# A second MoE computed in two phases over all tokens, both by seven block products

## The chip, the cores and the metric

One core of one Trainium2 chip. The metric is the time of the device in microseconds, as the median of several executions. TensorE (PE) multiplies, with a stationary operand of at most 128 x 128 and a moving operand of at most 512 columns; VectorE (DVE) and ScalarE (ACT) work element by element; SyncE (SP) issues every transfer here, on one queue.

## The reference

Inputs are x (8 batches, 8 heads, 512 tokens, 64 features), 32 states per batch and head, and weights.

```
attention: xread = softmax(x state^T / 8) state      512 rows per batch and head
           sread = softmax(state x^T / 8) x           32 rows per batch and head
tokens  = both by batch: 8 x (512 + 32) = 4352 rows of 512 features
first MoE:  h = relu(tokens @ w_in)  (512 x 2048);   y = (h * h) @ w_out
second MoE: xn = y / sqrt(mean(y*y) + 1e-6) * rms_g
            g = xn @ w_gate;  v = xn @ w_val          (512 x 1536 each)
            out = (g * sigmoid(g) * v) @ w_out2       (1536 x 512)
```

The weights arrive as float64 and are turned into float32 on the chip. A float32 product runs as three float32r passes: each operand is split into hi and lo = value - hi, and hi*hi + hi*lo + lo*hi are accumulated in PSUM.

## The kernel before

Tokens are features by tokens on chip: 128 features on the partitions, tokens in the columns. There are nine blocks: the 512 tokens of each batch, and the 256 states of all batches together (the state block, `SB`). A chunk is 128 hidden features.

**Order.** Every step is put at a position with `put(pos, fn, ...)`, and all steps are issued sorted by position. The unit is one chunk of an MoE loop. Positions that are not fixed by the loops come from the table `T`. Each engine works through its instructions in this order, and waits inside a step hold up what stands behind it on that engine. SP's transfers are one queue in the same order.

**Buffers.** On-chip buffers are 54 slots of 4 KB per partition (`u(...)`, one [128, 2, 512] float32 each); a slot is used again when the last reader of its old tile is done. PSUM has eight banks, four under the tag "mm" and four under "acc"; each holds 512 float32 per partition.

**First MoE** (L441 to L532). `moe1_in` makes h of a chunk, ScalarE applies Relu and Square, and the result is split: hi by a VectorE copy at L467, lo by a subtraction at L468. `moe1_out` adds the chunk to four "acc" banks, 2.5 positions after the chunk's place. At the end of a block `moe1_fin0` copies the banks out, two on ScalarE (L494) and two on VectorE (L495); `moe1_sq`, `moe1_rms`, `moe1_rinv` and `moe1_norm` make the normalized tokens, which are stored to DRAM (`xn_dr`). During a batch the attention of the next one is computed in steps in between. The weights of the second MoE are loaded and turned into float32 words during batches 1 to 7, and stored to DRAM as these.

**Second MoE** (L552 to L704). Gate and value of a chunk are one product of 2 x 2 blocks: rows of gate and value, halves of the 512 features, halves of the block's 512 tokens. Seven block products (Winograd's form of Strassen's algorithm) replace eight. Each is two 128-row blocks by three passes, with 256 tokens moving: 42 matmuls of 256 columns a chunk (`moe2_in`). ScalarE copies the first product, VectorE adds the others from PSUM (L646), then SiLU (L660), gate times value (L663) and the split of the result. `moe2_out` multiplies by w_out2 without block products: 4 token groups x 3 passes, 12 matmuls of 512 columns, one chunk later. The state block uses 24 matmuls of 256 columns and 6 of 512.

Weights for six of the twelve chunks are on chip at a time, so all blocks are gone through twice: `order` lists (half, block), the first half leaves partial sums in DRAM (`part_dr`), the second adds to them and stores the output (`moe2_fin`, L696).

```
    order = [(0, blk) for blk in (0, 1, 2, 3, SB, 4, 5, 6, 7)]
    order += [(1, blk) for blk in (7, 0, 1, 2, SB, 3, 4, 5, 6)]
```

Of the kernel before, what the change touches and what calls it, by code (L numbers as in the profile page):

```python
# [55 lines left out]
def attention_moe_kernel(  # L56
# [30 lines left out]
    NFH = NF2 // 2  # L87
# [9 lines left out]
    serial = [0]  # L97

# [59 lines left out]
    # A pair is two [128, 512] blocks of a weight; words holds it as float32 bits.  # L158
# [16 lines left out]
    def conv_a(key, j):  # L175
        if (key, j) not in raws:
            return
        t = raws[key, j]
        nc.scalar.activation(f(words[key][:, j, :]), f(t[:, :, 1]), AF.Abs, scale=2.0**-80)  # L179
        nc.scalar.activation(t[:, :, 0], t[:, :, 0], AF.Copy, bias=LOW_BIAS, scale=LOW_SCALE)  # L180

    def conv_b(key, j):
        if (key, j) not in raws:
            return
        t = raws.pop((key, j))
        w = words[key][:, j, :]
# [11 lines left out]
    def load_words(key):  # L198
        words[key] = u([P, 2, 512], U32, "wd")
        nc.sync.dma_start(f(words[key]), dram_words(key))  # L200

    his = {}

    def hi_words(key):
        his[key] = u([P, 2, 512], F32R, "wh")
        nc.scalar.copy(his[key], f(words[key]))
# [41 lines left out]
    def p_store(fq, bp, g):  # L248
        t = pst.pop((fq, bp, g))
# [7 lines left out]
    def load_p(b, fq):  # L257
        t = u([P, 2, 512], F32, "praw")
# [17 lines left out]
    def attn_steps(b):  # L276
# [38 lines left out]
        def s_pd(fq, g):  # L315
            """One batch's product with w_in by groups of heads, kept on chip."""
# [13 lines left out]
        def s_ex(g):  # L330
            t = st[g]
# [29 lines left out]
        def s_tokb(g):  # L361
            t = tk[g]
# [16 lines left out]
        def s_e2t(hc):  # L379
            ps = bank("mm", "e2p")  # L380
# [11 lines left out]
        def s_at(g):  # L392
            t = tk.pop(g)
# [5 lines left out]
        def s_sr(g):  # L399
            ps = bank("mm", "srp")  # L400
# [17 lines left out]
        def s_srt():  # L418
            ps = bank("mm", "srt")
# [21 lines left out]
    def moe1_in(blk, fc):  # L441
# [25 lines left out]
        nc.vector.tensor_copy(t[:, 0, :n], rg[:, 1, :n])  # L467
# [21 lines left out]
    def moe1_fin0(blk):  # L489
        n = ntok[blk]  # L490
# [8 lines left out]
    def moe1_sq(blk):  # L499
        n = ntok[blk]  # L500
# [10 lines left out]
    def moe1_rms(blk):  # L511
        n = ntok[blk]
# [6 lines left out]
    def moe1_rinv(blk, h):  # L519
        n = ntok[blk] // 2  # L520
# [3 lines left out]
    def moe1_norm(blk, j):  # L524
        n = ntok[blk]
# [12 lines left out]
    wsp = {}  # L538
    wtmp = {}
    w2 = {}  # L540
    xload = {}
    xtmp = {}
    xsp = {}
    part = {}
    part_dr = [
        dram.tile([P, ntok[k] // P, DM], F32, tag=f"part{k}", name=f"part_dr{k}")
        for k in range(NB)
    ]
    W_NAMES = ("a11", "a12", "a22", "s1", "s2", "s3", "s4")
    X_NAMES = ("b11", "b21", "b22", "t1", "t2", "t3", "t4")  # L550
# [4 lines left out]
    def load_w(c2):  # L555
        load_words(("wg", c2))
        load_words(("wv", c2))

    def sums_w(c2):
        g = f(words.pop(("wg", c2)))  # L560
        v = f(words.pop(("wv", c2)))
        t = [u([P, 2, 512], F32, "ws") for _ in range(2)]
        s1, s2, s3, s4 = t[0][:, 0, :], t[0][:, 1, :], t[1][:, 0, :], t[1][:, 1, :]
        a11, a12, a21, a22 = g[:, 0, :], g[:, 1, :], v[:, 0, :], v[:, 1, :]
        nc.vector.tensor_tensor(s1, a21, a22, op=ALU.add)
        nc.vector.tensor_tensor(s3, a11, a21, op=ALU.subtract)
        nc.vector.tensor_tensor(s2, s1, a11, op=ALU.subtract)
        nc.vector.tensor_tensor(s4, a12, s2, op=ALU.subtract)
        wtmp[c2] = dict(a11=a11, a12=a12, a22=a22, s1=s1, s2=s2, s3=s3, s4=s4)

    def split_w(c2, name):
        src = wtmp[c2].pop(name)
        t = u([P, 2, 512], F32R, "wq")
        split(src, t[:, 0, :], t[:, 1, :])
        wsp[c2, name] = quads(t)

    def load_xn(blk, j):
        t = u([P, 2, 512], F32, "xld")
        nc.sync.dma_start(t[:, :, : ntok[blk]], xn_dr[blk][:, 2 * j : 2 * j + 2, :])
        xload[blk, j] = t  # L580

    def sums_x(blk):
        x1, x2 = xload.pop((blk, 0)), xload.pop((blk, 1))
        b11, b21 = x1[:, :, :256], x2[:, :, :256]
        if blk == SB:
            t = u([P, 2, 256], F32, "xt4")
            nc.vector.tensor_tensor(t, b21, b11, op=ALU.subtract)
            xtmp[blk] = dict(b11=b11, b21=b21, t4=t)
            return
# [374 lines left out]
```

## Time and profile before

| | |
|---|---|
| time, median of 3 runs | 1525.35 us (1524.79 to 1525.41) |
| span of the profiled execution (its own time between first and last instruction) | 1524.0 us |
| TensorE busy | 1492.9 us, 98% |
| TensorE weight loads busy | 1327.7 us, 87% |
| VectorE busy | 1162.4 us, 76% |
| ScalarE busy | 734.6 us, 48% |
| transfers | 165 MB, mean 108 GB/s |
| granted TensorE clock, mean | 0.991 of full |

A busy share is the part of the span in which at least one instruction of the engine ran. Matmuls overlap, so the duration of one is longer than the distance from one to the next. In a list of groups the columns are: line, engine, operation, tiles written and read, shape and count, then busy time, mean of one in ns, and the idle time of the engine before them with what ended it. The first MoE runs to about 713 us, the second from there to the end; the first 60 us hold the first loads and conversions.

### The profile page before, as it was taken

What the parts mean: (1) busy time and instruction counts of PE and PEld (TensorE: products, weight loads), DVE (VectorE), ACT (ScalarE), POOL (GpSimd) and SP (SyncE); (2) the same over time, 40 slices, a digit from 0 to 9 for tenths busy, and PEclk for the clock granted to TensorE, in tenths of its full rate; (3) what the DMA queues carried; (4) which work ended last, traced back from release to release, by engine and by line L of the source; (5) the groups of instructions that cost most, each with busy time, mean ns of one, the idle gap of its engine ahead of it and who ended that gap; (6) DMA issues with size and microseconds to landing.
All of it is one profiled execution on the core that took longest, in us unless ns stands there. A gap on an engine that the chain in (4) does not pass through costs nothing.

```text
span 1524.0 us, 22599 instructions
## 1 busy us (share of the span) xinstructions
PE 1492.9 (98%) x8858; PEld 1327.7 (87%) x8858; DVE 1162.4 (76%) x2186; ACT 734.6 (48%) x1263; POOL 0.7 (0%) x6
## 2 busy tenths in 40 slices
PE   4999999999999999999999999999999999999998
PEld 2788888888888888889899999999999999999998
DVE  7997788888888989678886655778677776576674
ACT  5998666667666667654532323334332332232231
POOL 0000000000000000000000000000000000000000
PEclk6999999999999999999999999999999999999999
DMA  8976251515251534313021102012312022212100
GB/s 316 366 229 216 95 201 70 214 57 212 84 206 64 215 108 180 139 42 112 14 70 56 42 30 83 31 53 75 121 55 83 15 84 70 83 48 78 56 28 29
DMA packets 54971, 165.04 MB, mean 108 GB/s; under 512 B 6224, under 2 KB 7760, under 8 KB 54864
## 3 DMA queue, kind: packets, MB, share of 16 engines
q1 hardware_dynamic: 54864, 163.60, 30.7%
q8 instruction: 69, 1.13, 0.3%
q14 instruction: 38, 0.31, 0.1%
HBM read 109.58 MB, written 54.00 MB: 107 GB/s over the span
## 4 chain that ended last, share of the span: by engine, by line
PE 93%; ACT 3%; DVE 3%; issue 0%; DMA 0%; ACTq 0%; DVEq 0%
PE o L118 14%; PE o L119 14%; PE o L120 14%; PE x L120 10%; PE x L119 10%; PE x L118 10%; PE h L119 4%; PE h L118 4%; PE h L120 4%; ACT pst L246 1%; PE pps L118 1%; PE pps L120 1%; PE pps L119 1%; ACT wd L179 1%; ACT raw L180 1%; PE srp L120 1%
## 5 line engine op out<-in xcount | busy, mean ns | idle before, releaser
L118 PE MATMUL x<-xs,wq 128*128 128x256 f32 x1344 | 380.0, 283 | 0.5 <-ACT sq L517 0.4
L120 PE MATMUL x<-xs,wq 128*128 128x256 f32 x1344 | 380.3, 283 | 0.0
L119 PE MATMUL x<-xs,wq 128*128 128x256 f32 x1344 | 380.3, 283 | 0.0
L118 PEld LDWEIGHTS x<-xs,wq 128*128 128x128 f32 x1344 | 257.6, 192 | 4.5 <-ACT sq L517 0.6
L119 PEld LDWEIGHTS x<-xs,wq 128*128 128x128 f32 x1344 | 257.6, 192 | 3.6
L120 PEld LDWEIGHTS x<-xs,wq 128*128 128x128 f32 x1344 | 257.6, 192 | 0.0
L118 PE MATMUL o<-hl,wh 128*128 128x512 f32 (+1 forms) x576 | 217.7, 378 | 0.0
L119 PE MATMUL o<-hl,wh 128*128 128x512 f32 (+1 forms) x576 | 217.4, 377 | 0.0
L120 PE MATMUL o<-hl,wl 128*128 128x512 f32 (+1 forms) x576 | 217.4, 377 | 0.0
L660 ACT ACTIVATE rg<-rg 128x512 f32<-128x512 f32 x96 | 60.7, 632 | 319.6 <-DVE rg L646 319.6
L646 DVE TENSOR_TENSOR q<-q,x 128x256 f32<-128x256 f32 x288 | 112.3, 417 | 92.5 <-ACT q L649 58.3
L646 DVE TENSOR_TENSOR rg<-q,x 128x256 f32<-128x256 f32 x384 | 147.0, 417 | 25.8 <-PE x L120 25.3
L118 PE MATMUL o<-wh,hl 128*128 128x512 f32 x408 | 160.2, 393 | 1.0 <-ACT x L494 1.0
L119 PE MATMUL o<-wl,hl 128*128 128x512 f32 x408 | 160.0, 392 | 0.0
L120 PE MATMUL o<-wh,hl 128*128 128x512 f32 x408 | 158.7, 389 | 0.0
L115 DVE TENSOR_TENSOR hl<-rg,hl 128x512 fp32r<-128x512 f32 (+1 forms) x108 | 71.6, 663 | 71.6 <-ACT hl L114 71.6
L120 PEld LDWEIGHTS o<-hl,wl 128*128 128x128 f32 x576 | 108.4, 188 | 20.1
L118 PEld LDWEIGHTS o<-hl,wh 128*128 128x128 f32 x576 | 108.4, 188 | 19.8
L119 PEld LDWEIGHTS o<-hl,wh 128*128 128x128 f32 x576 | 108.4, 188 | 19.6
L464 ACT ACTIVATE rg<-h 128x512 f32<-128x512 f32 (+1 forms) x144 | 82.2, 571 | 83.1 <-PE h L120 82.9
L114 ACT CAST hl<-rg 128x512 fp32r<-128x512 f32 (+1 forms) x108 | 64.4, 597 | 91.1 <-DVE rg L663 72.8
L118 PE MATMUL h<-at,ph 128*128 128x512 f32 x256 | 101.5, 397 | 2.7 <-ACT pst L246 2.7
(154 smaller groups left out, 2592.1 us busy)
## 6 DMA issues: line engine op xcount, KB each, us to landing
raw<-in_moe_w_out_dram SPq DMA_DIRECT2D x30, 512.0 KB, 8.9
xld<-xn_dr SPq DMA_DIRECT2D x30, 512.0 KB, 5.7
p_dr<-pst SPq DMA_DIRECT2D x56, 256.0 KB, 4.6
praw<-p_dr SPq DMA_DIRECT2D x28, 512.0 KB, 4.2
xr<-in_x_t_dram SPq DMA_DIRECT2D x16, 512.0 KB, 6.0
raw<-in_moe_w_in_dram SPq DMA_DIRECT2D x16, 512.0 KB, 9.6
x<-in_x_n_dram SPq DMA_DIRECT2D x16, 512.0 KB, 8.4
xn_dr<-x SPq DMA_DIRECT2D x16, 512.0 KB, 3.3
```

The costliest lines, as they stand in the source:

```text
L114: nc.scalar.copy(hi, src)
L115: nc.vector.tensor_tensor(lo, src, f(hi), op=ALU.subtract)
L118: nc.tensor.matmul(ps, lh, rh, start=start, stop=False)
L119: nc.tensor.matmul(ps, lh, rl, start=False, stop=False)
L120: nc.tensor.matmul(ps, ll, rh, start=False, stop=stop)
L179: nc.scalar.activation(f(words[key][:, j, :]), f(t[:, :, 1]), AF.Abs, scale=2.0**-80)
L180: nc.scalar.activation(t[:, :, 0], t[:, :, 0], AF.Copy, bias=LOW_BIAS, scale=LOW_SCALE)
L246: nc.scalar.copy(pst[fq, bp, g][:, q, :], ps)
L464: nc.scalar.activation(rg[:, 0, :n], ps[:, :n], AF.Relu)
L646: add = lambda o, a, ps: nc.vector.tensor_tensor(o, a, ps, op=ALU.add)
L660: nc.scalar.activation(rg[:, 0, :], rg[:, 0, :], AF.Silu)
```

## The change

Gate and value are now computed for all tokens first (phase one), and the output product for all tokens after that (phase two).

- Phase one goes over pairs of batches `s`: the token halves of the 2 x 2 product are two batches of 512 tokens, so that each product has 512 moving columns. A pair of column blocks (`c2`, 256 gate and value columns) is loaded, summed and split, from DRAM: 7 tiles of 512 KB, for each pair of batches again. The state block follows each chunk of the last pair.
- Results of two chunks are summed for the left side of the output product (`h_sums`) and stored in DRAM as seven blocks (`h_store`).
- Phase two does the output product by seven block products too: blocks of two chunks by two halves of the 512 output features, for the tokens of two batches. It needs seven PSUM banks, accumulated over six pairs of chunks. The split w_out2 stays on chip (24 tiles).
- Sums and splits of all three weights are made during the first MoE (`wq_sums`, `wq_split`, `w2_sums`, `w2_split`) and stored in DRAM ready to use.
- In the first MoE the hi copy at L467 goes to ScalarE for all blocks but the first, the output products of batches 1 to 7 are issued one chunk later, and the last output products of the state block are drawn closer together.
- `after(step, *needs)` asserts while the program is written that a step stands behind those it needs, norm and its reciprocals among them; it issues nothing. The positions in `T` are others throughout, those of the start and of the attention by small amounts, and the norm's second half is now put behind both reciprocals with more distance (`rinv1` 5.05, `norm1` 6.1; before 4.48 and 5.18).

```diff
 def moe1_in(blk, fc):
 ...
-        nc.vector.tensor_copy(t[:, 0, :n], rg[:, 1, :n])
+        (nc.scalar.copy if blk else nc.vector.tensor_copy)(t[:, 0, :n], rg[:, 1, :n])
 ...
+    def recombine(k, ps, x, y):
+        add = lambda o, i, p: nc.vector.tensor_tensor(o, i, p, op=ALU.add)
+        if k == 0:
+            nc.scalar.copy(x[0], ps)
+        elif k == 1:
+            add(x[1], x[0], ps)
+        elif k == 2:
+            add(y[0], x[1], ps)
+        elif k == 3:
+            add(x[1], x[1], ps)
+            add(y[1], y[0], ps)
 ...
+    def wq_split(c2, m):
+        after(("wq", c2, m))
+        t = wsum[c2][m]
+        n = 1 if m == 3 else None
+        hi = hi_of(t, n)
 ...
+        lo = lo_of(t, hi)
+        nc.sync.dma_start(wq_dr[c2, 2 * m], f(hi))
+        nc.sync.dma_start(wq_dr[c2, 2 * m + 1], f(lo))
 ...
+    def moe2_in(s, fc, k):
+        a, b = PRODUCTS[k]
 ...
+        ps = any_bank("p") if s or fc else bank("mm", "p")
+        hi, lo = xq[s, b]
+        for j in range(2):
+            w_hi, w_lo = wq_part(fc // 2, a, j, cols)
+            mm3(ps, w_hi, w_lo, hi[:, j, :], lo[:, j, :], j == 0, j == 1)
+        recombine(k, ps, (x[:, 0, :], x[:, 1, :]), (y[:, 0, :], y[:, 1, :]))
+        if k == 5:
+            nc.scalar.activation(x, x, AF.Silu)
+        if k == 6:
+            nc.vector.tensor_tensor(y, x, y, op=ALU.mult)
 ...
+    def h_store(s, m):
 ...
+        for j in range(3):
+            nc.sync.dma_start(d[:, 2 * j : 2 * j + 2, :], t[j])
+        nc.sync.dma_start(d[:, 6, :], t[3][:, 0, :])
 ...
+    def load_hb(blk, m):
 ...
+        nc.sync.dma_start(t[0], hq_dr[s, m][:, :4, cols])
+        nc.sync.dma_start(t[1][:, :3, :], hq_dr[s, m][:, 4:, cols])
 ...
+    def moe2_out(blk, m, k):
 ...
+        if m == 0:
+            acc2[blk, k] = any_bank("o2")
 ...
+        for c in range(2):
+            o = ps[:, 256 * c : 256 * c + 256]
 ...
+            mm(hi[:, cols], w_hi, m == 0 and c == 0, False)
+            mm(hi[:, cols], w_lo, False, False)
+            mm(lo[:, cols], w_hi, False, last)
 ...
+            lag = LAG1 + (1 if 0 < blk < SB else 0)
+            put(blk * NF1 + fc + lag + 0.5 - late * (1 - T["tail"]), moe1_out, blk, fc)
+        e = (blk + 1) * NF1 + (lag - 1 if blk < SB else (LAG1 - 0.45) * T["tail"] - 0.54)
         put(e + 0.55, moe1_fin0, blk)
 ...
+    for s in range(B // 2):
+        e = n1 + s * NF2
+        for fc in range(NF2):
+            for k in range(7):
+                put(e + fc + k / 7, moe2_in, s, fc, k)
+            if s == B // 2 - 1:
+                put(e + fc + 0.95, moe2_in_sb, fc)
+            if fc % 2:
+                put(e + fc + 1 + T["hsum"], h_sums, s, fc // 2)
+                put(e + fc + 1 + T["hst"], h_store, s, fc // 2)
+            else:
 ...
+                    put(e + fc + T["wq0" if first else "wq"] + T["wq_gap"] * q, load_wq, fc // 2, m)
 ...
+    for fc in range(NF2):
+        put(n2 + fc / 2, moe2_out_sb, fc)
 ...
+    for blk in range(B):
+        e = n2 + (blk + 1) * nout
+        for m in range(nout):
+            for k in range(7):
+                put(e + m + k / 7, moe2_out, blk, m, k)
+            put(e + m + T["hbl"], load_hb, blk, m)
```

The positions that the steps above use: `hsum=0.3, hst=1.47, wq=-1.9, wq_gap=0.27, xsum=-4.63, xsp=-3.3, xsp_gap=0.44, hbl=-3.88, tail=0.3`.

## Rows read from the trace of the kernel before

**Rows 1.** The page: span, busy time (share) and instructions, and the transfers' mean rate.
```profile
span 1524.0 us, 22599 instructions
PE 1492.9 (98%) x8858; PEld 1327.7 (87%) x8858; DVE 1162.4 (76%) x2186; ACT 734.6 (48%) x1263; POOL 0.7 (0%) x6
...
DMA packets 54971, 165.04 MB, mean 108 GB/s; under 512 B 6224, under 2 KB 7760, under 8 KB 54864
```
**Rows 2.** The chain that ended last, shares of the span by engine.
```profile
PE 93%; ACT 3%; DVE 3%; issue 0%; DMA 0%; ACTq 0%; DVEq 0%
```
**Rows 3.** Waits of TensorE: total us, times, longest us.
```profile
PE pd L118 <- ACT wh L206: 8.0, 2, 5.8
PE stp L118 <- ACT xth L114: 6.8, 1, 6.8
```
**Rows 4.** Windows at the change to the second MoE: us, busy (instructions), clock, DMA share, GB/s.
```profile
720.00:730.00 10.00, 9.16 (x77) 8.96 (x75) 6.20 (x15) 3.04 (x6) 0.00 (x0) 1.00 0.16 52
...
750.00:760.00 10.00, 9.55 (x69) 8.86 (x68) 8.11 (x15) 6.95 (x11) 0.00 (x0) 1.00 0.01 2
```
**Rows 5.** TensorE in order of time, one chunk: start us, duration us.
```profile
1001.01 0.28 PE L118 MATMUL x<-xs,wq 128*128 128x256 f32 x1
...
1006.05 0.40 PE L118 MATMUL o<-wh,hl 128*128 128x512 f32 x1
...
1008.79 0.28 PE L118 MATMUL x<-xs,wq 128*128 128x256 f32 x1
```
**Rows 6.** TensorE's groups by form.
```profile
L118 PE MATMUL x<-xs,wq 128*128 128x256 f32 x1344 | 380.0, 283 | 0.5 <-ACT sq L517 0.4
...
L118 PE MATMUL o<-wh,hl 128*128 128x512 f32 x408 | 160.2, 393 | 1.0 <-ACT x L494 1.0
```
**Rows 7.** Groups by form of VectorE and of ScalarE.
```profile
L467 DVE CAST hl<-rg 128x512 fp32r<-128x512 f32 x128 | 54.2, 423 | 42.6 <-ACT rg L465 42.1
...
L115 DVE TENSOR_TENSOR xtl<-xr,xth 128x1024 fp32r<-128x1024 f32 x16 | 19.0, 1219 | 3.3 <-ACT xth L114 3.3
L696 DVE TENSOR_TENSOR pt<-pt,o 128x512 f32<-128x512 f32 x30 | 18.9, 681 | 0.6 <-PE o L120 0.6
...
L495 DVE COPY x<-o 128x512 f32<-128x512 f32 x16 | 10.4, 686 | 0.7 <-PE o L120 0.4
L596 DVE TENSOR_TENSOR xq<-xld,xq 128x512 f32<-128x512 f32 x15 | 10.4, 692 | 0.5
...
L505 DVE TENSOR_TENSOR sq<-sq,sq 128x1024 f32<-128x1024 f32 x8 | 9.8, 1225 | 3.2 <-ACT sq L504 3.2
...
L506 DVE TENSOR_TENSOR sq<-sq 128x256 f32<-128x256 f32 x1 | 0.4, 424 | 0.0
...
L114 ACT CAST hl<-rg 128x512 fp32r<-128x512 f32 x96 | 59.6, 621 | 72.8 <-DVE rg L663 72.8
...
L114 ACT CAST xth<-xr 128x1024 fp32r<-128x1024 f32 x16 | 16.2, 1051 | 3.1 <-DMA xr<-in_x_t_dram 3.1
```
**Rows 8.** Window of one batch of the first MoE, between equal instructions of two batches.
```profile
431.67:504.25 72.58, 72.58 (x338) 60.56 (x337) 63.13 (x110) 47.58 (x75) 0.00 (x0) 1.00 0.39 142
```
**Rows 9.** Windows with busy transfers (last two columns: DMA share, GB/s).
```profile
50.00:150.00 100.00, 99.20 (x440) 80.57 (x439) 86.22 (x141) 89.91 (x158) 0.00 (x0) 1.00 0.78 257
...
10.00:20.00 10.00, 3.39 (x10) 2.08 (x9) 9.58 (x16) 7.51 (x13) 0.00 (x0) 0.70 1.03 410
...
50.00:60.00 10.00, 9.54 (x41) 7.28 (x40) 9.21 (x15) 9.94 (x19) 0.00 (x0) 1.00 1.01 361
60.00:70.00 10.00, 10.00 (x45) 8.01 (x44) 9.74 (x16) 9.97 (x18) 0.00 (x0) 1.00 0.99 307
...
870.00:872.00 2.00, 2.00 (x17) 1.95 (x16) 1.64 (x6) 0.17 (x1) 0.00 (x0) 1.00 0.99 265
```
**Rows 10.** The end, in order of time: the last additions on VectorE.
```profile
1517.60 2.74 DVE L696 TENSOR_TENSOR pt<-pt,o 128x512 f32<-128x512 f32 x4 [0.63 <-PE o L120]
```
**Rows 11.** A 512 KB load: count, KB, median us from issue to landing.
```profile
xld<-xn_dr SPq DMA_DIRECT2D x30, 512.0 KB, 5.7
```

More of the change, by code (lines that the diff above doesn't have):

```diff
@@ L97, in attention_moe_kernel, with after @@
     serial = [0]
+    steps_done = set()
+    def after(step, *needs):
+        for need in needs:
+            assert need in steps_done, (step, need)
+        steps_done.add(step)
     def u(shape, dt, name):
@@ L202, in attention_moe_kernel @@
     his = {}
+    his_reload = set()
     def hi_words(key):
+        if sources[key[0]].dtype != F32 and key not in his_reload:
+            after(("hi", key), ("b", key, 0), ("b", key, 1))
         his[key] = u([P, 2, 512], F32R, "wh")
@@ L248, in p_store @@
     def p_store(fq, bp, g):
+        after(("pst", fq, bp, g))
         t = pst.pop((fq, bp, g))
@@ L330, in s_ex @@
         def s_ex(g):
+            after(("ex", b, g))
             t = st[g]
@@ L361, in s_tokb @@
         def s_tokb(g):
+            after(("tokb", b, g))
             t = tk[g]
@@ L392, in s_at @@
         def s_at(g):
+            after(("at", b, g), ("tokb", b, g))
             t = tk.pop(g)
@@ L399, in s_sr @@
         def s_sr(g):
+            after(("sr", b, g))
             ps = bank("mm", "srp")
@@ L489, in moe1_fin0 @@
     def moe1_fin0(blk):
+        after(("fin0", blk))
         n = ntok[blk]
@@ L499, in moe1_sq @@
     def moe1_sq(blk):
+        after(("sq", blk), ("fin0", blk))
         n = ntok[blk]
@@ L511, in moe1_rms @@
     def moe1_rms(blk):
+        after(("rms", blk), ("sq", blk))
         n = ntok[blk]
@@ L524, in moe1_norm @@
     def moe1_norm(blk, j):
+        after(("norm", blk, j), ("rinv", blk, 0), ("rinv", blk, 1))
         n = ntok[blk]
@@ L532, in moe1_norm @@
         nc.sync.dma_start(xn_dr[blk][:, 2 * j : 2 * j + 2, :], x2[j][:, :, :n])
[L538 to L550, printed above, removed]
+    PRODUCTS = (
+        ("a11", "b11"), ("s2", "t2"), ("s3", "t3"), ("s1", "t1"),
+        ("a12", "b21"), ("s4", "b22"), ("a22", "t4"),
+    )
@@ new lines, in attention_moe_kernel, with sums_left @@
+    wq_dr = {
+        (c2, m): dram.tile([P, 2, 512], F32, tag=f"wq{c2}_{m}", name=f"wq_dr{c2}_{m}")
+        for c2 in range(NF2 // 2)
+        for m in range(7)
+    }
+    wsum = {}
+    def sums_left(g, v):
+        t = [u([P, 2, 512], F32, "sa") for _ in range(2)]
+        s1, s2, s4 = t[0][:, 0, :], t[0][:, 1, :], t[1][:, 0, :]
+        sub = lambda o, i, j: nc.vector.tensor_tensor(o, i, j, op=ALU.subtract)
+        nc.vector.tensor_tensor(s1, v[0], v[1], op=ALU.add)
+        sub(s2, s1, g[0])
+        sub(v[0], g[0], v[0])
+        sub(s4, g[1], s2)
+        return t
@@ new lines, in attention_moe_kernel, with load_wq, wq_part @@
+    W_AT = dict(a11=(0, 0), a12=(0, 1), s3=(1, 0), a22=(1, 1), s1=(2, 0), s2=(2, 1))
+    wq = {}
+    def load_wq(c2, m):
+        after(("ldwq", c2, m), ("wq", c2, m // 2))
+        wq[c2, m] = u([P, 2, 512], F32R, "wq")
+        nc.sync.dma_start(f(wq[c2, m]), wq_dr[c2, m])
+    def wq_part(c2, name, k, cols):
+        if name == "s4":
+            t = quads(wq[c2, 6])
+            return t[:, 0, k, cols], t[:, 1, k, cols]
+        m, j = W_AT[name]
+        return tuple(quads(wq[c2, 2 * m + i])[:, j, k, cols] for i in range(2))
@@ L682, in moe2_fin @@
[L682 to L704 removed]
+    xb = {}
@@ new lines, in split_xb @@
+    def split_xb(s, name):
+        if (s, name) not in xb:
+            return
+        t = xb.pop((s, name))
+        if s == SB:
+            n = ntok[SB]
+            hi = u([P, 2, 512], F32R, "hi")
+            nc.scalar.copy(hi[:, :, :n], f(t)[:, :, :n])
+            lo = u([P, 2, 512], F32R, "lo")
+            nc.vector.tensor_tensor(lo[:, :, :n], f(t)[:, :, :n], f(hi)[:, :, :n], op=ALU.subtract)
+        else:
+            hi = hi_of(t)
+            lo = lo_of(t, hi)
+        xq[s, name] = (hi, lo)
@@ new lines, in moe2_in_sb, with product @@
+    def moe2_in_sb(fc):
+        cols = slice((fc % 2) * P, (fc % 2 + 1) * P)
+        n = ntok[SB]
+        g, v = any_bank("g")[:, :n], any_bank("v")[:, :n]
+        def product(ps, a, b, first):
+            hi, lo = xq[SB, b]
+            for j in range(2):
+                w_hi, w_lo = wq_part(fc // 2, a, j, cols)
+                start, stop = first and j == 0, not first and j == 1
+                mm3(ps, w_hi, w_lo, hi[:, j, :n], lo[:, j, :n], start, stop)
+        product(g, "a11", "b11", True)
+        product(g, "a12", "b21", False)
+        product(v, "s1", "b11", True)
+        product(v, "a22", "t4", False)
+        q, r = divmod(fc, 4)
+        if r == 0:
+            hs[q] = u([P, 4, 256], F32, "hs")
+        t = u([P, 2, 512], F32, "rg")
+        nc.scalar.activation(t[:, 0, :n], g, AF.Silu)
+        nc.vector.tensor_tensor(hs[q][:, r, :], t[:, 0, :n], v, op=ALU.mult)
@@ new lines, in h_sums @@
+    def h_sums(s, m):
+        h0, h1 = hg.pop((s, 2 * m)), hg.pop((s, 2 * m + 1))
+        t = [u([P, 2, 512], F32, "sa") for _ in range(2)]
+        s1, s2, s4 = t[0][:, 0, :], t[0][:, 1, :], t[1][:, 0, :]
+        a11, a21, a12, a22 = h0[:, 0, :], h0[:, 1, :], h1[:, 0, :], h1[:, 1, :]
+        sub = lambda o, i, j: nc.vector.tensor_tensor(o, i, j, op=ALU.subtract)
+        nc.vector.tensor_tensor(s1, a21, a22, op=ALU.add)
+        sub(s2, s1, a11)
+        sub(a21, a11, a21)
+        sub(s4, a12, s2)
+        hg[s, m, "out"] = (h0, h1, t[0], t[1])
@@ new lines, in h_store, with w2_sums @@
+    def h_store(s, m):
+        after(("hst", s, m))
+        d = hq_dr[s, m]
+        t = hg.pop((s, m, "out"))
+        for j in range(3):
+            nc.sync.dma_start(d[:, 2 * j : 2 * j + 2, :], t[j])
+        nc.sync.dma_start(d[:, 6, :], t[3][:, 0, :])
+    w2_dr = {
+        (m, i): dram.tile([P, 2, 512], F32, tag=f"w2_{m}_{i}", name=f"w2_dr{m}_{i}")
+        for m in range(NF2 // 2)
+        for i in range(4)
+    }
+    w2s = {}
+    w2q = {}
+    def w2_sums(m):
+        after(("w2sum", m), ("b", ("w2", m), 0), ("b", ("w2", m), 1))
+        w = words.pop(("w2", m))
+        b = f(w)
+        b11, b12, b21, b22 = b[:, 0, :256], b[:, 0, 256:], b[:, 1, :256], b[:, 1, 256:]
+        t = u([P, 4, 256], F32, "tw")
+        sub = lambda o, i, j: nc.vector.tensor_tensor(o, i, j, op=ALU.subtract)
+        sub(t[:, 0, :], b12, b11)
+        sub(t[:, 2, :], b22, b12)
+        sub(t[:, 1, :], b22, t[:, 0, :])
+        sub(t[:, 3, :], b21, t[:, 1, :])
+        w2s[m] = (w, t.rearrange("p (a q) m -> p a (q m)", a=2))
@@ new lines, in w2_part @@
+    def w2_part(m, name):
+        i, q = B_AT[name]
+        return tuple(
+            w2q[m, i + j].rearrange("p a (q m) -> p (a q) m", q=2)[:, q, :] for j in range(2)
+        )
+    hb = {}
+    def load_hb(blk, m):
+        s, ob = divmod(blk, 2)
+        cols = slice(256 * ob, 256 * ob + 256)
+        after(("ldhb", blk, m), ("hst", s, m))
+        t = [u([P, 4, 256], F32, "hb"), u([P, 4, 256], F32, "hc")]
+        nc.sync.dma_start(t[0], hq_dr[s, m][:, :4, cols])
+        nc.sync.dma_start(t[1][:, :3, :], hq_dr[s, m][:, 4:, cols])
+        hb[blk, m] = t
@@ new lines, in split_hb @@
+    def split_hb(blk, m, i):
+        t = hb[blk, m][i]
+        n = 4 - i
+        hi, lo = u([P, 4, 256], F32R, "hh"), u([P, 4, 256], F32R, "hl")
+        split(t[:, :n, :], hi[:, :n, :], lo[:, :n, :])
+        hb[blk, m][i] = (hi, lo)
+    acc2 = {}
+    def moe2_out(blk, m, k):
+        a, b = PRODUCTS[k]
+        last = m == NF2 // 2 - 1
+        if m == 0:
+            acc2[blk, k] = any_bank("o2")
+        ps = acc2[blk, k]
+        i, q = divmod(A_ROW.index(a), 4)
+        hi, lo = (t[:, q, :] for t in hb[blk, m][i])
+        w_hi, w_lo = w2_part(m, b)
+        for c in range(2):
+            o = ps[:, 256 * c : 256 * c + 256]
+            cols = slice(c * P, (c + 1) * P)
+            mm = lambda l, r, start, stop: nc.tensor.matmul(
+                o, l, r, start=start, stop=stop, skip_group_check=True
+            )
+            mm(hi[:, cols], w_hi, m == 0 and c == 0, False)
+            mm(hi[:, cols], w_lo, False, False)
+            mm(lo[:, cols], w_hi, False, last)
+        if not last:
+            return
+        if k == 0:
+            acc2[blk] = [u([P, 2, 512], F32, "ox"), u([P, 2, 512], F32, "oy")]
+        ox, oy = acc2[blk]
+        pv = ps.rearrange("p (c d) -> p c d", c=2)
+        recombine(k, pv, (ox[:, :, :256], ox[:, :, 256:]), (oy[:, :, :256], oy[:, :, 256:]))
+        s, ob = divmod(blk, 2)
+        for i, done in ((0, 5), (1, 6)):
+            if k == done:
+                b = 2 * s + i
+                rows = out[b * NT : b * NT + S, :].rearrange("(p c) m -> p c m", c=4)
+                nc.sync.dma_start(rows[:, 2 * ob : 2 * ob + 2, :], acc2[blk][i])
@@ new lines, in split_hs, with moe2_out_sb @@
+    def split_hs(q):
+        hi, lo = u([P, 4, 256], F32R, "hh"), u([P, 4, 256], F32R, "hl")
+        split(hs[q], hi, lo)
+        hs[q] = (hi, lo)
+    def moe2_out_sb(fc):
+        if fc == 0:
+            acc2[SB, 0], acc2[SB, 1] = any_bank("o2"), any_bank("o2")
+        q, r = divmod(fc, 4)
+        hi, lo = hs[q]
+        w_hi, w_lo = w2q[fc // 2, 0][:, fc % 2, :], w2q[fc // 2, 1][:, fc % 2, :]
+        for c in range(2):
+            cols = slice(c * P, (c + 1) * P)
+            mm3(acc2[SB, c], hi[:, r, cols], lo[:, r, cols], w_hi, w_lo, fc == 0, fc == NF2 - 1)
+        if fc < NF2 - 1:
+            return
+        t = u([P, 2, 512], F32, "os")
+        nc.scalar.copy(t[:, 0, :], acc2[SB, 0])
+        nc.vector.tensor_copy(t[:, 1, :], acc2[SB, 1])
+        for c in range(2):
+            for q in range(4):
+                r0 = (4 * c + q) * NT + S
+                nc.sync.dma_start(out[r0 : r0 + NS, :], t[32 * q : 32 * q + 32, c, :])
@@ L800, in attention_moe_kernel @@
+    for m in range(nout):
+        for i in range(4):
+            put(n2 + T["w2l"] + T["w2l_gap"] * m + T["w2l_i"] * i, load_w2, m, i)
     halves = ("xt", "st", "toka", "tokb", "at", "ex", "r2", "e2t", "xn", "sr")
```

327 lines of the change are left out of this document (136 added, 191 removed).

## The prediction

> **What bounds the kernel now.** I read the page's busy line first: the reader is to see TensorE busy for 98% of the span, VectorE for 76%, ScalarE for 48% [rows 1]. The chain that ended last lies on TensorE for 93% of the span [rows 2], so time is won only by giving that engine fewer or shorter matmuls. What it ever waited for is in the waits: the long ones belong to the first 60 us (8.0 us for a split of w_in, 6.8 us for the first tokens) [rows 3], and of the second MoE's products only 0.5 us stands in their group [rows 6]. Where one stage goes over into the other, the ten-microsecond windows show 0.84 and 0.45 us without a matmul [rows 4].
>
> The busy time of one matmul (283 ns, 393 ns) is no price, since matmuls overlap; a sequence in order of time gives it [rows 5]. From the first 256-column product at 1001.01 us to the first of 512 columns at 1006.05 us there are 42 matmuls: 0.120 us each. From there to 1008.79 us there are 12: 0.2283 us each. Two of 256 columns therefore cost 0.240 us where one of 512 costs 0.2283.
>
> **TensorE, the term that decides.** In the kernel before, gate and value of the eight batches are 96 chunks (8 batches by 12) of 7 products x 2 blocks x 3 passes at 256 columns: 4032 matmuls, as 3 x 1344 in the groups [rows 6]. Times 0.120 that is 483.8 us. The output product takes 96 x 4 x 3 = 1152 at 512 columns (the 3 x 408 of the group less 72 of the state block): 263.0 us. The changed kernel works on pairs of batches: 48 chunks x 42 matmuls = 2016 at 512 columns, 460.3 us. Its output product is 8 x 6 x 7 products x 2 halves x 3 passes = 2016 at 256 columns, 241.9 us. The state block keeps its 288 and 72 matmuls. Sum: 702.2 - 746.8 = **-44.6 us**. Had the price been purely by columns, 73,728 columns fewer at 0.2283/512 us would give -32.9 us; that is the other end. I take -44.6, because both lengths are read from the stage that changes.
> The Trainium skill ("TensorE: Matmul & The Clock Gate", section "Wait — 56ns, not 53.3ns?") gives a warm matmul N/2.4 GHz plus about 2.5 ns, 109 and 216 ns here, by which the sum would be -33.7 us; the trace shows 120 and 228 ns, 13 to 15 ns over N/2.4 at a granted clock of 1.00 [rows 8], and decides.
>
> **First MoE: what moves in.** The weights of the second MoE are now summed, split and stored in split form during batches 1 to 7, where before only their float32 words were stored. Per batch and per pair of columns VectorE gets 4 sums of 512 (0.69 each), 4 of 256 (0.42), five differences of 1024 (1.22) and one of 512 (0.69): 11.2 us; the copy at L467, 16 x 0.423 = 6.8 us, goes to ScalarE [rows 7]. Net +4.5 us on 63.1 us of a 72.58 us batch [rows 8]: 93%. ScalarE gets 16 x 0.621 + 5 x 1.05 + 0.62 = 15.8 us on 47.6 us [rows 7, 8]: 87%. The output products of these batches are issued one chunk later, which gives their chain of copies 4 us more. The stores grow from 3 to 11 of 512 KB per batch, +4.2 MB or 58 GB/s on some 142. I cost all this at nothing, since TensorE, at 100% there, covers it; what it costs if that cover is gone is a rival below.
> One new wait I see in the positions: with its longer delay, batch 7's copies out of PSUM (fin0, 130.55) stand behind the state block's first output product (130.5), which needs the same four banks. TensorE waits for two copies on each of ScalarE and VectorE (0.686 us each on VectorE [rows 7]), and every matmul is queued behind it. Between one copy and four in a row: 0.7 to 2.7 us. I take **+1.5**.
> The first loads and conversions keep their order but for small shifts (two of the four state loads change places). The longest single waits there are 5.8 and 6.8 us [rows 3]; I take 0, within 4 either way. At the change of stages the norm's steps of the state block and the preparation of 1024 tokens (4 x 1.225 + 7 x 1.22 = 13.4 us of VectorE) stand where sums and splits of weights and tokens stood: 0, within the 1.3 us lost there now [rows 4].
>
> **Phase one: gate and value.** A chunk lasts 42 x 0.2283 = 9.59 us. VectorE needs for it 7 additions out of PSUM at 512 columns (0.681), one product of 1024 (1.225), and half of four sums (1.38): 7.37 us; with the next pair's preparation, spread over 12 chunks, 8.49 us or 89% [rows 7]. Inside the 4.4 chunks where that preparation stands it is 32.4 + 13.4 = 45.8 us for 42.2, a backlog of some 4 us. Eight PSUM banks, used in turn, let it fall six products (8 us) behind before TensorE stops, so I charge only **+1.5** over the three seams between pairs, from 0 to 6.
> Transfers are the term that grows most. Each of the six column pairs is loaded anew for each of the four pairs of batches: 24 times 7 x 0.524 MB come in and 1.84 MB of results go out. With inputs, and three quarters of the 12.6 MB of w_out, 144.6 MB fall into 460.3 + 34.6 (state block) = 494.9 us: 292 GB/s, against 108 over the whole run now [rows 1]; in the first three pairs 35.1 MB in 115 us, 305 GB/s. The trace of before has windows at full share with 410, 361 and 307 GB/s, and with 1 KB rows 265 [rows 9]. The first two leave room, the third just does. Loads stand 0.8 to 1.9 chunks (8 to 18 us) ahead, so I price them at nothing while 300 GB/s are had.
>
> **Phase two: output.** A block of hidden features lasts 42 x 0.120 = 5.04 us; the splits of 1024 and 768 columns take VectorE 2.2 us of it and ScalarE 1.9. It loads 0.92 MB in 1 KB rows, 182 GB/s, below the 265 of such rows [rows 9]. Its beginning is tight: the last results can be stored only about 2 us after phase one ends, then 1.84 MB of them, two parts of w_out and the first 0.92 MB to come back are one queue on SP: 3.8 MB at 361 GB/s is 10.5 us [rows 9], some 4 us more to land (a 512 KB load lands 5.7 us after its issue [rows 11], its own bytes take 1.5), 2.3 us to split, 18.8 us; the state block's output products cover 72 x 0.2283 = 16.4 us. **+2** (0 to 6). The end is unchanged: one addition of 0.7 us (as the last of four in 2.74 us now [rows 10]) and one store of 512 KB behind the last matmul.
>
> Sum: -44.6 + 1.5 + 1.5 + 2 = -39.6 us on the profiled execution's 1524.0 us [rows 1], 1484.4 us; the median of the runs lies 1.35 us above that span, so **1486 us**.
>
> **The rivals.**
> A. The price goes by columns, not by matmuls: 1497 us. For it: a pipelined engine might hide a fixed cost. Against it: both lengths are measured back to back, 2 x 0.120 > 0.2283.
> B. The first MoE becomes bound by VectorE and ScalarE. VectorE has 9.4 us idle per batch, and new work takes 4.5 of them [rows 8]. If its idle time, much of it spent waiting for ScalarE, cannot be used, each of six batches grows by 4.5 us: +27, 1513 us. Against it: TensorE showed no wait there at 87% VectorE, and the added delay.
> C. Phase one is starved here and there, by loads landing late or by buffers (of 54 slots some 49 are in use at a seam: 28 by the split tokens of two pairs, 14 by weights, 7 by results and sums). At 5.7 us, one landing [rows 11], for two to six of the 24 changes of column pair, 11 to 34 us come back: 1497 to 1520 us. For it: 305 GB/s wanted and 307 seen leave nearly no room. Against it: the loads stand 8 to 18 us ahead.
> D. On the other side: the one DMA queue sets phase one. It decides from 144.6 MB / (494.9 + 39.6) = 270 GB/s; below that the kernel is slower than before. At 257 GB/s, the rate of the busiest 100 us after the first 50 [rows 9], phase one lasts 563 us, +68: 1554 us. For it: loads and stores mixed have not been kept above 307 for long. Against it: the share there was 0.78, so it was not the queue's limit.
>
> **How the numbers follow.** The forecast, 1474 to 1496, has 56%; A 6%, B 11%, C 11%, D 12%, and 4% for less than 1474 (a better start). The likeliest is 1486. The range takes A, B and C in and leaves D and the good end out, 16%: 1474 to 1521. Measurement tells 0.2%, about 3 us, from no change: faster holds the forecast, the good end, A and most of B and C, 0.83; same 0.04 (stalls that eat the whole gain); slower 0.13, D and the end of B.
>
> **What would show it.** Right: matmuls of phase one 0.228 us apart and 42 to a chunk of 9.6 us; output blocks of 5.04 us; TensorE at 100% in windows of batches 2 to 7; a short wait of an "o" matmul for copies near 670 us; a GB/s near 300 in phase one with TensorE still busy. Wrong: chunks longer than 9.6 us with TensorE waiting for DMA (D, C) or for VectorE; batches longer than 72.6 us (B); 512-column matmuls more than 0.235 us apart. The prediction as a whole falls if phase one lasts over 530 us.

## The result, and the profile after

The changed kernel takes 1485.4 us (median), 0.9745 of the kernel before (95% interval 0.973 to 0.976): faster, and 0.6 us from the forecast of 1486. Beside the experiments it was run again: 1487.0 us, ratio 0.9747 (0.9733 to 0.976). The profiled span fell from 1524.0 [rows 1] to 1482.6 us, by 41.4.

The page of the changed kernel, with the lines that answer to [rows 1]:

```profile
span 1482.6 us, 20652 instructions
PE 1447.2 (98%) x7706; PEld 1248.6 (84%) x7706; DVE 1125.2 (76%) x1654; ACT 783.0 (53%) x1186; POOL 0.7 (0%) x6
...
DMA packets 138420, 345.82 MB, mean 233 GB/s; under 512 B 12112, under 2 KB 56144, under 8 KB 138320
```

TensorE still sets the time, with 1152 fewer matmuls (8858 to 7706), and the transfers have doubled. Its waits outside the first 60 us are short (us in total, times, longest), as in [rows 3]:

```profile
PE p L126 <- DVE hx L594: 2.0, 1, 2.0
PE o L126 <- DVE x L518: 0.8, 2, 0.7
PE o L859 <- ACT hh L122: 0.8, 1, 0.8
PE o L859 <- DVE hl L123: 0.8, 1, 0.8
```

TensorE in order of time in phase one; from the first of these to the second there are fourteen times three matmuls:

```profile
761.81 0.39 PE L126 MATMUL p<-hi,wq 128*128 128x512 f32 x1
...
771.33 0.39 PE L126 MATMUL p<-hi,wq 128*128 128x512 f32 x1
```

That is 9.52 us for the 42 of a chunk, 0.2267 us each. Phase two, and what stands before it, in the chain that ended last (start us, us, what):

```profile
1224.56 7.99 DMA hb<-hq_dr
...
1232.63 1.05 ACT hh L122
...
1233.71 1.24 DVE hl L123
...
1234.99 241.38 PE o L859 x2008
```

2008 matmuls of 256 columns in 241.38 us are 0.1202 us each. In windows of the changed kernel (us, busy times, clock, DMA share, GB/s) one batch of the first MoE, which answers to [rows 8], the first three pairs of phase one, and phase two:

```profile
330.30:403.36 73.06, 72.93 (x337) 60.39 (x336) 66.17 (x107) 61.77 (x98) 0.00 (x0) 1.00 0.55 198
...
719.00:833.00 114.00, 112.01 (x507) 92.94 (x507) 92.10 (x131) 31.14 (x40) 0.00 (x0) 1.00 0.73 281
833.00:948.00 115.00, 115.00 (x509) 95.27 (x508) 95.24 (x131) 25.73 (x32) 0.00 (x0) 1.00 0.81 306
948.00:1063.00 115.00, 115.00 (x509) 95.27 (x508) 96.09 (x132) 26.62 (x32) 0.00 (x0) 1.00 0.78 291
...
1235.00:1476.00 241.00, 241.00 (x2007) 240.91 (x2008) 131.50 (x149) 88.95 (x103) 0.00 (x0) 1.00 0.65 210
```

A batch has become 0.5 us longer, VectorE is busy for 66.2 us of it (63.1 before) and ScalarE for 61.8 (47.6). For the first three pairs 305 GB/s had been worked out; they moved 281, 306 and 291, with TensorE at 100% in the second and the third.

### The profile page after: what moved, and what is told of

Same layout as the page of the kernel before. It is cut to its first block, busy times and chain, and to the rows that moved or that the text cites. A ratio compares the mean times of both kernels' runs of the same rounds, so it can differ in the third digit from the quotient of the medians.

```text
span 1482.6 us, 20652 instructions
## 1 busy us (share of the span) xinstructions
PE 1447.2 (98%) x7706; PEld 1248.6 (84%) x7706; DVE 1125.2 (76%) x1654; ACT 783.0 (53%) x1186; POOL 0.7 (0%) x6
## 5 line engine op out<-in xcount | busy, mean ns | idle before, releaser
L126 PE MATMUL p<-hi,wq 128*128 128x512 f32 x672 | 261.7, 389 | 2.0 <-DVE hx L594 2.0
L127 PE MATMUL p<-lo,wq 128*128 128x512 f32 x672 | 261.6, 389 | 0.0
L128 PE MATMUL p<-hi,wq 128*128 128x512 f32 x672 | 261.4, 389 | 0.0
L859 PE MATMUL o<-w,hh 128*128 128x256 f32 x1344 | 242.1, 283 | 0.8 <-ACT hh L122 0.8
L859 PEld LDWEIGHTS o<-w,hh 128*128 128x128 f32 x1344 | 209.6, 192 | 1.3 <-ACT hh L122 1.3
L859 PE MATMUL o<-w,hl 128*128 128x256 f32 x672 | 190.4, 283 | 0.8 <-DVE hl L123 0.8
L594 DVE TENSOR_TENSOR hx<-hx,p 128x512 f32<-128x512 f32 x192 | 128.9, 683 | 52.6 <-PE p L128 49.6
L126 PEld LDWEIGHTS p<-hi,wq 128*128 128x128 f32 x672 | 126.2, 188 | 28.2 <-DVE hx L594 2.4
L128 PEld LDWEIGHTS p<-hi,wq 128*128 128x128 f32 x672 | 126.2, 188 | 26.4
L127 PEld LDWEIGHTS p<-lo,wq 128*128 128x128 f32 x672 | 126.2, 188 | 25.5
L859 PEld LDWEIGHTS o<-w,hl 128*128 128x128 f32 x672 | 129.0, 192 | 1.1 <-DVE hl L123 1.0
L123 DVE TENSOR_TENSOR hl<-hb,hh 128x1024 fp32r<-128x1024 f32 x48 | 58.7, 1222 | 57.1 <-ACT hh L122 57.1
```

The source lines that it names most:

```text
L123: nc.vector.tensor_tensor(lo, src, f(hi), op=ALU.subtract)
L126: nc.tensor.matmul(ps, lh, rh, start=start, stop=False)
L127: nc.tensor.matmul(ps, lh, rl, start=False, stop=False)
L128: nc.tensor.matmul(ps, ll, rh, start=False, stop=stop)
L594: add = lambda o, i, p: nc.vector.tensor_tensor(o, i, p, op=ALU.add)
L859: mm = lambda l, r, start, stop: nc.tensor.matmul(o, l, r, start=start, stop=stop, skip_group_check=True)
```

## The experiments

Gains and losses are given by the profiled span against 1482.6 us, unless a median is named.

**half_columns**: each product of phase one in two halves (`pairs` holds the weight tiles, hi and lo, of both blocks `j`).

```diff
-            mm3(ps, w_hi, w_lo, hi[:, j, :], lo[:, j, :], j == 0, j == 1)
 ...
+        for c in range(2):
+            o = slice(256 * c, 256 * c + 256)
+            for j, (w_hi, w_lo) in enumerate(pairs):
+                mm3(ps[:, o], w_hi, w_lo, hi[:, j, o], lo[:, j, o], j == 0, j == 1)
```

> Phase one's products run as two halves of 256 columns each instead of one of 512, with the same sums, loads and element work: 4032 matmuls in place of 2016. Theory (each matmul costs some 13 ns beside its columns, and TensorE sets phase one): 4032 x 0.120 = 483.8 us in place of 2016 x 0.2267 = 457.0 us, a chunk of 10.1 us in place of 9.5, VectorE gets slack so the 2.0 us wait at the first seam goes: +25 to +27 us over the changed kernel, span near 1508. Rival (the price goes by columns): within 2 us of the changed kernel. Rival (the one DMA queue or VectorE sets phase one): less than +15, as TensorE's longer work hides behind them.

Measured: 1510.2 us (ratio 0.990, 0.9883 to 0.9916), span 1507.0, +24.4, just under the +25 to +27 of the theory. The products of the changed kernel, then of this one (count of one of three passes, first and last start):

```profile
L126 PE MATMUL p<-hi,wq x672: 389/389/468, 719.2 to 1212.8; 128*128 128x512 f32 x168
```
```profile
L126 PE MATMUL p<-hi,wq x1344: 282/283/355, 719.3 to 1237.8; 128*128 128x256 f32 x192
```

Phase one grew from 493.6 to 518.5 us, and the wait of 2.0 us went: 26.9 us for 2016 more matmuls, 13.3 ns each. The price by columns (rival A) falls, and phase one is set by TensorE.

**store_twice_part** and **store_twice**: results of phase one are stored a second time, in part or all. These are the lines of the first; the second has `range(3)` and the seventh block as well.

```diff
+        d = hq2_dr[s, m]
+        for j in range(2):
+            nc.sync.dma_start(d[:, 2 * j : 2 * j + 2, :], t[j])
```

> Two of the four result stores of each pair of chunks in phase one are made twice, the second time to a DRAM tensor that nobody reads: 24 x 1.05 = 25.2 MB more, 169.8 MB in the 497 us of phase one, 342 GB/s. Theory (the queue keeps near 400 GB/s, so there is room): within +4 us. Rival (the queue's limit in this mix of loads and stores is 307 GB/s, as in the window of before at full share): phase one takes 553 us, +56 us.

> All four result stores of each pair of chunks are made twice, 44 MB more, 188.6 MB in phase one, 380 GB/s. Theory (near 400 GB/s): the mean still fits but little is left for loads that come late, +0 to +20 us. Rival with a limit of 361 GB/s: 522 us, +25 us. Rival with a limit of 307 GB/s: 614 us, +117 us.

Measured: 1498.4 us (0.9821, 0.9807 to 0.9836), span 1495.8, +13.2; and 1510.5 us (0.9899, 0.9884 to 0.9913), span 1506.9, +24.3. The first lies between its theories. The second lies just above mine, and by its size alone it would fit the rival with a limit of 361 GB/s, +25. Against that limit stands the second pair of phase one in store_twice, which moved more:

```profile
833.00:948.00 115.00, 115.00 (x509) 95.24 (x508) 95.24 (x131) 25.97 (x31) 0.00 (x0) 1.00 1.02 407
```

407 GB/s at full share, with TensorE at 100%: the queue carries a third more than the change asks for, and in this pair even that costs nothing. The loss lies in a few waits: from 800 us on they sum to 20.6 us in store_twice against 3.6 in the changed kernel, at 812 us (5.8, where the changed kernel has its 2.0), at 1006 (1.2), early in the fourth pair at 1086 (3.3) and at the start of phase two at 1256 (10.3). Behind the long ones the granted clock is lower, 0.70 in 810 to 820 us and 0.52 in 1250 to 1260. Waits of TensorE in store_twice, and in store_twice_part with two of its windows:

```profile
PE o L868 <- ACT hh L122: 9.8, 1, 9.8
PE p L126 <- DMA wq<-wq_dr: 9.1, 2, 5.8
```
```profile
PE o L867 <- ACT hh L122: 5.6, 1, 5.6
...
PE p L126 <- DVE lo L588: 4.4, 1, 4.4
```
```profile
810.00:820.00 10.00, 7.48 (x26) 6.04 (x27) 5.02 (x7) 2.54 (x4) 0.00 (x0) 0.83 1.03 415
...
1246.00:1249.00 3.00, 2.54 (x12) 2.24 (x12) 2.32 (x3) 1.54 (x3) 0.00 (x0) 0.50 1.09 349
```

From 1240 us TensorE stands for 5.6 us, waiting for the first results to come back; behind the wait the granted clock is 0.50, the lower of its two levels, and from 1250.2 us on three matmuls take 0.36 us again. Of the 13.2 us, 6.1 lie behind phase one, 4.5 in it and 2.6 ahead of it, all between 257 and 626 us in the first MoE, whose program is unchanged. Rival D, a queue that sets the whole phase, falls; loads that land late at a few places (rival C) are what more traffic would buy.

**copy_on_vector**: the hi copy of the first MoE back on VectorE.

```diff
-        (nc.scalar.copy if blk else nc.vector.tensor_copy)(t[:, 0, :n], rg[:, 1, :n])
+        nc.vector.tensor_copy(t[:, 0, :n], rg[:, 1, :n])
```

> The hi copy in the first MoE stays on VectorE in all blocks. Theory (VectorE has room for the new weight work only because this copy left it): 63.1 + 11.2 = 74.3 us of work per batch of 73.1 us, with its waits 75 to 79 us per batch for the six batches that prepare weights, +12 to +35 us. Rival (there is cover enough either way): +0 to +2 us.

Measured: 1511.5 us (0.9906, 0.9891 to 0.9921), span 1509.8, +27.2, inside the theory. One matmul of the norm stands once per batch, here 78.66 us from the next; TensorE waits for VectorE's copies out of PSUM:

```profile
339.08 0.40 PE L540 MATMUL ms<-sqr,ones 128*128 128x512 f32 x1
...
417.74 0.40 PE L540 MATMUL ms<-sqr,ones 128*128 128x512 f32 x1
```
```profile
PE o L126 <- DVE x L518: 11.5, 6, 2.5
...
PE h L126 <- ACT at L122: 3.8, 5, 0.8
```

All of the loss lies ahead of phase one, whose first product starts 27.5 us later. Behind the four longest waits, 2.4 to 2.5 us each, TensorE goes on at the lower clock, as here:

```profile
480.00:490.00 10.00, 7.52 (x29) 5.85 (x28) 9.90 (x14) 6.43 (x9) 0.00 (x0) 0.83 0.41 134
```

That clock makes little of the loss: one of the four executions had a mean clock of 0.991, no lower than the changed kernel's, and took 1509.7 us; the others took 1510.9 to 1512.6 at 0.985 and 0.986.

**no_extra_lag**: output products of the first MoE at their old distance. The copies out of PSUM and the norm at a block's end are placed by the same `lag`, so in batches 1 to 7 they move a chunk earlier too.

```diff
-            lag = LAG1 + (1 if 0 < blk < SB else 0)
+            lag = LAG1
```

> The output products of batches 1 to 7 are issued 2.5 positions after their chunk in place of 3.5; all else is the changed kernel. Theory (with the copy on ScalarE the chain Relu, Square, copy, difference is 2.5 us of work on engines that are 85 to 91% busy, and the later place covers what it waits for): TensorE waits for VectorE before output products in the batches that prepare weights, 0.5 to 2.5 us per batch, +3 to +15 us. Rival (9 us of distance are cover enough): within 2 us.

Measured: 1508.0 us (0.9887, 0.9874 to 0.9901), span 1506.3, +23.7, half as much again as my upper end. A batch takes 77.4 us. The wait that was expected, for the difference (`hl`), is 9.6 us of it; the theory did not name the copies out of PSUM (5.0) and ScalarE's steps of the attention (4.7). The waits of TensorE:

```profile
PE o L127 <- DVE hl L490: 9.6, 7, 1.7
...
PE o L126 <- DVE x L518: 5.0, 6, 1.0
PE e2p L402 <- ACT st L354: 4.7, 5, 0.9
```

Two small edits of the first MoE thus keep 24 to 27 us each: without either, more than half of the change's gain would be gone.

**changed_again** is the changed kernel beside the next ones; **results_first** queues the first load of phase two earlier; **both_seams** also moves the norm of the state block (the lines behind `...`, which stand in place of the four with `T` alone).

```diff
-            put(e + m + T["hbl"], load_hb, blk, m)
+            put(e + m + (-4.55 if blk == 0 and m == 0 else T["hbl"]), load_hb, blk, m)
 ...
+        last = blk == SB
+        put(e + (3.6 if last else T["rinv0"]), moe1_rinv, blk, 0)
+        put(e + (4.0 if last else T["rinv1"]), moe1_rinv, blk, 1)
+        put(e + (5.4 if last else T["norm0"]), moe1_norm, blk, 0)
+        put(e + (4.6 if last else T["norm1"]), moe1_norm, blk, 1)
```

> The changed kernel itself, run beside the next three for comparison: 1485.4 us as before, span 1482.6.

> The first load of phase two (results of the first pair of chunks, stored 400 us earlier) is queued ahead of the store of the last results instead of behind it. Theory (the 1.6 us that TensorE loses at 1233 us are this load's 8.0 us of landing behind 1.84 MB of stores and two parts of w_out): that wait goes, -1.5 to -2.5 us. Rival (another load, of w_out or of the next results, is late at once): less than 1 us won.

> As the one before, and the state block's reciprocals and norm are placed 0.6 to 1.8 chunks earlier, ahead of the sums that prepare the second pair. Theory (the 2.0 us wait at 805 us is VectorE's backlog, to which the norm's 1.8 us add): that wait falls to under 0.5 us, -3 to -4.5 us in all, near 1481.5 us. Rival (the backlog is the four sums of 1.22 us alone): the wait stays over 1.5 us, and only the gain of the kernel before this one is left.

Measured: changed_again span 1483.9; results_first 1482.5 us (0.972, 0.9706 to 0.9733), span 1481.7; both_seams 1483.8 us (0.9724, 0.9711 to 0.9737), span 1482.0. Waits of TensorE at phase two's start in changed_again, then in results_first:

```profile
PE o L859 <- ACT hh L122: 0.9, 1, 0.9
PE o L859 <- DVE hl L123: 0.8, 1, 0.8
```
```profile
PE o L859 <- DVE hl L123: 0.5, 1, 0.5
```

The first theory named the wait rightly: 0.5 us of 1.7 is left. From the first product of phase one to the end 761.7 us pass in place of 763.1, so 1.4 us were won, just short of its range. In both_seams the 2 us wait went from its place, and one of 0.7 came at 788 us; against changed_again that is -1.9 by the span, short of what the second theory gave, and -3.2 by the median, its low end. But the trace spoke against its reason. In changed_again the same wait, at the same matmul, has another name:

```profile
808.73 0.47 PE L126 MATMUL p<-hi,wq 128*128 128x512 f32 x1 [1.57 <-DMA wq<-wq_dr]
```

The addition on VectorE that ends the wait by name in the first profile, the first one behind the four sums, ends there at 807.44 us, just before TensorE goes on at 807.49. In this execution it is still running when TensorE goes on at 808.73. It stands below as in the first profile, then as in this one:

```profile
806.76 0.68 DVE L594 TENSOR_TENSOR hx<-hx,p 128x512 f32<-128x512 f32 x1
```
```profile
808.43 0.68 DVE L594 TENSOR_TENSOR hx<-hx,p 128x512 f32<-128x512 f32 x1
```

So TensorE did not need that addition. In both executions 366 matmuls of phase one lie ahead of the wait, eight chunks of 42 and five products of 6: the sixth product of the next chunk, the first that needs the last tile of the fifth column pair. In the first profile the transfers on SP, in order of time, show that tile's load as the first of the seven at 797.92, and the second fence its landing:

```profile
782.53 0.37 SPq L559 DMA_DIRECT2D xn_dr<-x  x1
782.99 1.86 SPq L657 DMA_DIRECT2D wq<-wq_dr  x4
793.50 0.37 SPq L559 DMA_DIRECT2D xn_dr<-x  x1
793.91 0.97 SPq L657 DMA_DIRECT2D wq<-wq_dr  x2
...
797.92 7.98 SPq L657 DMA_DIRECT2D wq<-wq_dr  x7
```
```profile
L657 SPq DMA_DIRECT2D wq<-wq_dr x1: 392/392/392, 797.9 to 797.9; - x1
...
DMA to landing us min/median/max: 9.4/9.4/9.4
```

797.9 + 9.4 = 807.3 us, and TensorE goes on at 807.49. SP had stood since 784.9 us at the norm's second store, which waited for VectorE until 793.50, with the weight loads behind it. The new theory moves only that store.

**store_later** and **store_later_results_first**:

```diff
-        nc.sync.dma_start(xn_dr[blk][:, 2 * j : 2 * j + 2, :], x2[j][:, :, :n])
+        if blk < SB:
+            norm_store(blk, j)
 ...
+        if blk == SB:
+            put(n1 + 9.9, norm_store, blk, 0)
+            put(n1 + 9.9, norm_store, blk, 1)
```

> The changed kernel with one move: the two stores of the state block's normalized tokens are queued at chunk 9.9 of the first pair, after all loads of the fifth column pair; VectorE's order is untouched. Theory (the 2 us wait in chunk 8 is the last weight tile of that column pair, landing 9.4 us after an issue that stood on SP behind the norm's second store, which waited for VectorE until 793.5 us): no wait of TensorE in chunk 8, -1.5 to -2.0 us, span near 1481. Rival (VectorE's backlog of the four sums and the norm holds the PSUM bank): the wait of 1.6 to 2.0 us stays, since VectorE's work and order are the same.

> The move of store_later and that of results_first together. Theory (two separate waits on SP's queue): both gains add, -3.5 to -4 us from the changed kernel's span, near 1479.5, and below both_seams by about 1 to 2 us. Rival (VectorE's backlog): no better than results_first, span 1481 to 1482.

Measured: 1484.5 us (0.9735, 0.9722 to 0.9749), span 1481.3; and 1482.4 us (0.9719, 0.9706 to 0.9733), span 1480.8. In store_later VectorE does the same work in the same order, and no wait is left in that stretch:

```profile
800.00:815.00 15.00, 15.00 (x68) 12.43 (x67) 13.97 (x18) 4.47 (x6) 0.00 (x0) 1.00 0.66 225
```

Phase one's products, 493.6 us in the changed kernel, take 491.4 in both kernels with the move; in store_later:

```profile
L126 PE MATMUL p<-hi,wq x672: 389/389/396, 718.6 to 1210.0; 128*128 128x512 f32 x168
```

The backlog theory falls, SP's queue is shown, by the traces: the medians of store_later and changed_again do not tell it, as their intervals overlap. Of store_later's 2.2 us only 0.7 reach the end. At phase two's start TensorE waits for 0.9 and 0.8 us in it as in the changed kernel, but here the granted clock then falls to 0.50, and the 17 matmuls from 1233.66 us on take about 1.5 us longer:

```profile
1234.00:1236.00 2.00, 2.00 (x12) 2.00 (x11) 1.13 (x1) 1.68 (x2) 0.00 (x0) 0.50 1.10 349
```

In the changed kernel it stays at 1.00 there. With both moves the span from the first product of phase one to the end is 760.2 us against 763.4, 3.2 us less, a little under what was expected; the first product itself lay at 718.6 to 721.0 us in these executions, which blurs a comparison of whole spans. By the medians store_later_results_first is the fastest here with results_first (1482.4 and 1482.5), and the intervals of the two overlap.

## Why the prediction was right, step by step

The forecast was -39.6 us, the spans gave -41.4, and the mechanism is the one named: TensorE sets the time, and its sequence got shorter. The terms, measured:

- *TensorE, -44.6*: right, too small. 2016 x 0.2267 + 2016 x 0.120 = 698.9 us against 96 x 7.78 = 746.9 [rows 5], -48.0. The 0.2283 us that I took for 512 columns came from twelve matmuls between others of 256 columns [rows 5] and holds the change from one to the other (the first three take 0.69 us, the next three 0.69, the last six 1.36); in a row of their own they take 0.2267. By 0.2267 and 0.120, a column costs 0.417 ns and a matmul 13.3 ns beside its columns: 73,728 columns fewer are 30.7 us of the 48.0, 1152 matmuls fewer 15.3, and the changes of length that are gone 2. The Trainium skill ("TensorE: Matmul & The Clock Gate", section "Wait — 56ns, not 53.3ns?") has about 2.5 ns for a warm matmul beside its columns. An estimate from that figure makes half_columns 2016 x 2.5 ns = 5 us slower. The runs show 13.3 ns and 26.9 us, and they decide here.
- *First MoE, 0*: cover held, with five batches 2.9 us longer (365.8 us from one norm to the sixth, 362.9 before), 1.1 us of it without a matmul, 0.9 of that in two waits for the copies out of PSUM at 468 and 541 us. The other 1.8 us no run explains. That both edits of the first MoE were needed for the cover is shown by copy_on_vector and no_extra_lag. That the first cost the +27 of rival B is chance: B priced 4.5 us a batch with the copy on ScalarE, and here VectorE had 11.2 more.
- *The wait before the state block, +1.5*: wrong, it was 0. The four banks come free one by one. Copies of the changed kernel on ScalarE and on VectorE:

```profile
678.48 0.58 ACT L517 COPY x<-o 128x512 f32<-128x512 f32 x1
679.37 0.59 ACT L517 COPY x<-o 128x512 f32<-128x512 f32 x1 [0.31 <-PE o L128]
```
```profile
679.06 0.69 DVE L518 COPY x<-o 128x512 f32<-128x512 f32 x1
680.05 0.69 DVE L518 COPY x<-o 128x512 f32<-128x512 f32 x1 [0.30 <-PE o L128]
```

  The last copy ends at 680.74 us, and the state block's first output products, which begin at 679.85, reach the fourth bank at 680.92. I had priced the copies as if the last bank were asked for first.
- *Change of stages, 0*: -1.5; the 1.5 us lost between 720 and 760 us before ([rows 4] has 1.3 of them) are gone.
- *Three seams, +1.5*: 2.0 us, near in size and wrong in kind. It came once, in the first pair alone, and it is not VectorE's backlog, but a weight load behind a store on SP that waits for VectorE: rival C's mechanism, at one of the 24 changes of column pair. I had placed the norm's steps on VectorE and not asked what their stores hold up.
- *Phase two's beginning, +2*: 1.6 us, by the load that was named: issued at 1224.56, landed after 8.0 us; results_first took most of it away. The first loads to come back ran at 349 GB/s at full share (1250 to 1260 us), so the 265 read from two microseconds [rows 9] was no limit of 1 KB rows.
- *Transfers, 0*: right but for that one load, and with more room than I could read: 306 GB/s wanted, 407 carried. The 144.6 MB were added up wrongly, their own terms give some 148; 140.5 MB moved between the first and the last product, 284 GB/s.
- *Start, 0*: the last matmul of the states' product starts at 151.1 us, 150.9 before. *End, 0*: 5.8 us from the start of the last matmul to the end, 4.8 before.

-48.0 + 2.9 - 1.5 + 2.0 + 1.6 + 1.0 = -42.0 of the -41.4; 0.6 us are not accounted for. The errors were of both signs, which is why the sum came closer than its terms, and that is luck. I had named a wait of 2 us nearly to size and for the wrong reason, and only a kernel that moved the store alone told the two apart.

## What to carry to other kernels

Price matmuls by their start-to-start distance in a sequence of their own kind: two of 256 columns cost 13 ns more than one of 512, and 1152 matmuls fewer were 15 us here beside what their columns cost. When a step moves, follow its store as well as its arithmetic: on a shared queue a store that waits for an engine holds every load behind it. Where an engine at 100% covers added work, take the cover away edit by edit: here one copy and one chunk of distance were worth 24 to 27 us each.

## What was not expected of the hardware

- The one queue carried 407 GB/s over 115 us in a mix of loads and stores while TensorE ran at 100%; the trace of before had shown at most 410 over ten [rows 9].
- The name of a wait can differ between two executions of one program: the same wait of TensorE, at the same matmul, stood as 2.0 us for VectorE and as 1.6 us for a weight load.
- A wait of 5.6 us cost more than itself: TensorE went on at a granted clock of 0.50 (1.2 GHz), where three matmuls of 256 columns take 0.64 us in place of 0.36, for some 4 us. Behind waits of 0.9 and 0.8 us the clock fell in store_later and stayed at 1.00 in the changed kernel.
